# First stage of an attention and MLP kernel: V and two query groups projected in small tiles on both halves of the rows, scores among them; clears behind the first inverse root

## The chip, the cores and the metric

The kernel runs on one core of a Trainium2 chip. The metric is the device time of one execution in microseconds (us). TensorE (PE) does the matrix products, ScalarE (ACT) activations and copies, VectorE (DVE) reductions and elementwise work, GpSimd (POOL) elementwise work, and SyncE (SP) issues the transfers. Each engine works through its own queue in order.

## The reference

```python
# S = 2048 rows, D = 512, 32 heads of 16, F = 1792
xn = layernorm(A_x)                        # (x - mean) / sqrt(var + 1e-5)
q, k, v = split_heads(xn @ A_wqkv)
p = softmax(q @ k.T * 16 ** -0.5)
attn = merge_heads(p @ v) @ A_wo
mlp = gelu(xn @ B_w1 + B_b1) @ B_w2 + B_b2
out = A_x + attn + mlp
```

## The kernel before

A product that must be exact to about float32 is made of three products of float16 pairs (high and low part of each factor), so a tile of 128 x 512 with D = 512 takes 4 x 3 = 12 matmuls. The work falls into a first stage, a loop of units, and an end.

**The unit loop.** One unit belongs to a group of four heads and 512 queries (16 units each) and covers 128 keys; there are 512 units. PE makes the scores of the four heads first with queries as the weights (S, 128 x 512 each), of which DVE takes the maximum over the keys (L392, four to a unit); 16 units give the row maxima m of the 512 queries. Later PE makes the scores again with keys as the weights and with the row maxima in added rows of the stacks (E), ACT takes the exponential of E (L433, four instructions of 128 x 512 to a unit), and PE multiplies by V. The S part runs 19 units (`LEAD`) ahead of E. All these matmuls are small tiles of 62 or 64 rows by 32 columns (helper at L171), several of which run side by side in the array, on two halves of its rows. On the half of the rows that P·V leaves free runs "dense" work: the projections of the later head groups, the remaining V tiles, then the MLP, then the output projection. The last V tiles (11 to 15) are the first of that dense work.

**The first stage**, which the change rewrites, prepares this. A class `Plan` is a list scheduler: `add` puts down a task with its engine, a guessed duration in ns, what it comes after, the buffers that it takes and frees, and a `tail` (how much work hangs behind it); `run` takes at each step, for the engine that can start first, the startable task with the longest tail, and so fixes the order of every engine's queue. Its guesses are used for nothing else. The tasks, with the lines of before:

- `tile_in` (L900): the 16 tiles of x, 128 x 512 each, into 8 buffers; tiles 8 to 15 wait until earlier ones have been transposed. `wq_in` (L909): the first weights of Q and K. `piece_in` (L915): weight pieces of 512 KB (`wch`, three buffers): two of V, then 18 pieces m0 to m17 of the MLP and output weights.
- `total` (L923): ACT sums a piece's absolute values, from which scale factors are worked out; it frees the piece's buffer. The totals of the 18 pieces have the lowest tail of all.
- `normal`: mean and variance (L972, L973), `sd` = var + eps (L974), a Sqrt on ACT (L976), a Newton step on DVE (L978 to L982), then x is normalised, two tiles of the first four on DVE (L990) and two on ACT (L987).
- `turned`: PE transposes (L1004), copies to float16 high parts on ACT (L1008), low parts on DVE or POOL (L1017, L1023).
- `twelve` (L1034): the 12 full 128 x 128 x 512 matmuls of one tile, in four chunks of three. `project0` does so for a K or Q group of 512 rows, copies the result (`stg`), stores it (`qk_d`) and loads it back in stacked form (`kst`, `qst`, L538).
- `score`: two tasks to a unit, each eight small matmuls into two banks, then two maxima of 128 x 512 on DVE (L392).
- `v_tile`: `twelve` for one of the first 11 (`NV`) V tiles, copied by ACT to `vv` (L1131).
- the row maxima of the first 16 units: a reduction on DVE (L358), three small steps on POOL (L360 to L362), a PE transpose (L366), a copy on ACT (L371), a store by SP (`m_d`, L347) and two loads into the rows of `qst` (`m_rows`, L352).
- POOL clears `kst`, `qst` of both sets and parts of `vv` at the very start (L90, L93, L94).

While PE has nothing to do, `fill` gives it matmuls whose results are not used (L1192).

Of the kernel before, what the change touches and what calls it, by code (L numbers as in the profile page):

```python
# [9 lines left out]
F32 = mybir.dt.float32  # L10
# [26 lines left out]
TAIL = 5  # L37
WARM = 430
NV = 11
LAG, E_TAIL = 3000, 9500  # L40
LANE = 225
WFROM, WSTEP, XN = 10, 4.5, 4.5
VT = 2600, -2000
WV_TAIL, WV_DVE = 50000, 2
# [11 lines left out]
def layer_kernel(ctx: ExitStack, tc: tile.TileContext, x, wqkv, wo, w1, b1, w2, b2, out):  # L56
# [30 lines left out]
    def clear(i, blocks=range(NQB)):  # L87
        for b in blocks:
            for st, v in ((kst, MROWS), (qst, 0.0)):
                nc.gpsimd.memset(st[i][b].rearrange("p h n -> p (h n)").bitcast(F32), v)  # L90

    vv = const.tile([P, NT, H * VW + 15], F32, name="vv")
    nc.gpsimd.memset(vv[:, :, 0:H * VW].rearrange("p t (h e) -> p t h e", e=VW)[:, :, :, DH], 1.0)  # L93
    nc.gpsimd.memset(vv[:, :, H * VW:], 0.0)  # L94
# [122 lines left out]
    class Plan:  # L217
# [3 lines left out]
        def __init__(self, **pools):  # L221
            self.todo, self.pools = [], {k: (n, []) for k, n in pools.items()}
            self.freed, self.slot, self.users = {}, {}, {}

        def add(self, engine, ns, fn, after=(), take=(), free=(), size=0, tail=0, gap=0):
            t = dict(gap=gap, e=engine, ns=ns, fn=fn, after=[a for a in after if a], take=take, free=free, size=size, tail=tail,
                     end=None, n=len(self.todo))
            for key in free:
                self.users.setdefault(key, []).append(t)
            self.todo.append(t)  # L230
            return t

        def late(self, a, t):
            return 60 if a["e"] == t["e"] else self.LATE[a["e"]]
# [16 lines left out]
        def run(self, fill):  # L251
            for t in reversed(self.todo):
                for a in t["after"]:
                    assert a["n"] < t["n"]
                    wire = LAG + a["size"] * 3 if a["size"] else 0
                    a["tail"] = max(a["tail"], t["tail"] + max(t["ns"] + self.late(a, t) + wire, t["gap"] if a["gap"] else 0))
            at = {"PE": 1200.0, "ACT": 2020.0, "DVE": 1200.0, "POOL": 4000.0, "SP": 740.0}
            wire, left = 0.0, list(self.todo)
            while left:
# [7 lines left out]
                s, t = max((c for c in can[e] if c[0] <= first[e] + 120), key=lambda c: (c[1]["tail"], -c[1]["n"]))  # L267
                if e == "PE":
                    fill(at[e], s)
                for key in t["take"]:  # L270
# [5 lines left out]
                if t["size"]:  # L276
                    wire = max(wire, at[e] + 1300) + t["size"] * 3
                    t["end"] = wire + 500
# [75 lines left out]
    def m_parts(t):  # L354

        mx = work.tile([P, 2, 8], F32, name="mx", bufs=1)
        parts = work.tile([P, 2, 2, 8], F16, name="mparts", bufs=2)
        return (lambda: nc.vector.tensor_reduce(mx.rearrange("p a r -> p (a r)"), mt_of[t].rearrange("p h t k -> p (h t) k"),  # L358
                                                axis=AX.X, op=ALU.max),
                lambda: nc.gpsimd.tensor_scalar(mx, mx, 1.0 / MROW, 0.0, op0=ALU.mult, op1=ALU.add),  # L360
                lambda: nc.gpsimd.tensor_scalar(parts[:, :, 0], mx, 1.0, 0.0, op0=ALU.mult, op1=ALU.add),
                lambda: nc.gpsimd.tensor_tensor(parts[:, :, 1], mx, parts[:, :, 0], op=ALU.subtract)), parts  # L362
# [238 lines left out]
    def split_qk(m, wf, inv, ready_w):  # L601
        wh = ph.tile([P, 2, 2, NC, P], F16, name="wqk_h", bufs=2)
        for w in (1, 0):
            assert (m, w) in here
# [234 lines left out]
    with ExitStack() as st1:  # L839
# [53 lines left out]
        def raw(key, tag, shape, bufs):  # L893
            tl[key] = (px if tag == "xs" else ph).tile(shape, F32, name=tag, bufs=bufs)
            return tl[key]

        def tile_in(t):
            def fn():
                xs[t] = raw(("xs", t), "xs", [P, D], 8)
                nc.sync.dma_start(xs[t], x[t * P:(t + 1) * P, :])  # L900
            return add("SP", 450, fn, take=[("xs", t)], size=256, tail=(300000 if t < 4 else 270000 if t < 8 else 0))
# [10 lines left out]
        def piece_in(key, src, after=(), tail=0):  # L912
# [3 lines left out]
            return add("SP", 420, fn, after, take=[key], size=700, tail=tail)  # L916

        def total(ns, key, dst, after, done=()):
# [5 lines left out]
            return add("ACT", ns, fn, [after], free=done)  # L924
# [25 lines left out]

        amq = work.tile([P, 2], F32, name="amq")
# [10 lines left out]
        n_last = []  # L962
        DVE_X, DVE_LO = (2, 2, 0, 0), (4, 4, 0, 0)

        def normal(sb):
# [10 lines left out]
            a = add("ACT", 200, lambda: nc.scalar.activation(sd[:, 1], sd[:, 0], AF.Sqrt), [a] + n_last)  # L976
            n_last[:] = [a]
            a = add("DVE", 90, lambda: nc.vector.tensor_tensor(sd[:, 2], sd[:, 1], sd[:, 1], op=ALU.mult), [a])  # L978
            a = add("DVE", 90, lambda: nc.vector.tensor_tensor(sd[:, 2], sd[:, 2], sd[:, 0], op=ALU.add), [a])
            a = add("DVE", 90, lambda: nc.vector.reciprocal(sd[:, 3], sd[:, 2]), [a])  # L980
            a = add("DVE", 90, lambda: nc.vector.scalar_tensor_tensor(sd[:, 2], sd[:, 1], 2.0, sd[:, 3], op0=ALU.mult, op1=ALU.mult), [a])
# [12 lines left out]
        def turned(sb, done):  # L994

            his, los = [], []
            for c in range(NC):
# [8 lines left out]
                t = add("PE", 440, turn, done, take=[key], free=[("xs", 4 * sb + i) for i in range(4)])  # L1006
# [31 lines left out]
        def project0(w, sb):  # L1038

            key, st = ("X", "p", w, sb), ("stg", w, sb)  # L1040
            p = twelve(key, [lambda c=c, i=i, j=j: (wqh[:, w, i, c, :], xt[:, j, c, sb * QB:(sb + 1) * QB])
                             for c in range(NC) for i, j in PAIRS], lambda c: [his[sb][c], los[sb][c], w_ready[w], t_last[sb]])
# [5 lines left out]
            h = add("ACT", 480, hi, [p], take=[st], free=[key])  # L1048
# [14 lines left out]
            for a_ in range(2):  # L1063
                got.append(add("SP", 420, lambda a_=a_: stack(0, w, sb, a_), [a, b], size=96))
# [464 lines left out]
```

## Time and profile before

| | |
|---|---|
| median of 3 runs | 1450.94 us (1450.76 to 1452.97) |
| profiled execution | 1450.07 us, its span 1448.3 us |
| PE, DVE, ACT, POOL busy | 99%, 93%, 87%, 47% of the span |
| first score matmul | 33.53 us |
| last score matmul of the first stage | 94.80 us |
| first exponential of the unit loop | 95.48 us |
| last exponential | 1431.5 us |

Rows of the timeline give start, duration, engine, line, operation, output<-input and count; in brackets stands the idle time of the engine before it and what ended it. "SPq" is the issue of a transfer, "PEld" a weight load. A table of stretches has the stretch, its length, busy time and count of each engine (PE, PEld, DVE, ACT, POOL, or only the one asked for), the granted PE clock, the share of the DMA engines and GB/s. A row of waits has the waiting engine and line, what it waited for, the us in total, the times, and the longest.

### The profile page before, as it was taken

What the parts mean: (1) busy time and instruction counts of PE and PEld (TensorE: products, weight loads), DVE (VectorE), ACT (ScalarE), POOL (GpSimd) and SP (SyncE); (2) the same over time, 40 slices, a digit from 0 to 9 for tenths busy, and PEclk for the clock granted to TensorE, in tenths of its full rate; (3) what the DMA queues carried; (4) which work ended last, traced back from release to release, by engine and by line L of the source; (5) the groups of instructions that cost most, each with busy time, mean ns of one, the idle gap of its engine ahead of it and who ended that gap; (6) DMA issues with size and microseconds to landing.
All of it is one profiled execution on the core that took longest, in us unless ns stands there. A gap on an engine that the chain in (4) does not pass through costs nothing.

```text
span 1448.3 us, 88564 instructions
## 1 busy us (share of the span) xinstructions
PE 1430.8 (99%) x40120; PEld 960.0 (66%) x40120; DVE 1350.1 (93%) x2240; ACT 1259.7 (87%) x2399; POOL 684.6 (47%) x769
## 2 busy tenths in 40 slices
PE   7999999999999999999999999999999999999998
PEld 3347676766666667666677766666766667666664
DVE  7979999999999999999999999999999999999933
ACT  5868888888999888999998889998889999888885
POOL 3301857663688511278742137884015778212110
PEclk9999999999999999999999999999999999999999
DMA  6741564555224111121113011121112210211423
GB/s 210 216 139 33 171 205 159 160 177 158 73 87 120 55 47 38 46 84 45 45 45 89 24 45 45 53 77 46 44 36 73 62 37 21 59 56 47 137 70 115
DMA packets 111474, 124.84 MB, mean 86 GB/s; under 512 B 21244, under 2 KB 83068, under 8 KB 111096
## 3 DMA queue, kind: packets, MB, share of 16 engines
q1 hardware_dynamic: 111096, 119.18, 27.2%
q8 instruction: 313, 5.13, 1.5%
q14 instruction: 65, 0.53, 0.1%
HBM read 81.66 MB, written 37.34 MB: 82 GB/s over the span
## 4 chain that ended last, share of the span: by engine, by line
PE 93%; DVE 4%; ACT 1%; DMA 1%; issue 0%; POOL 0%; DVEq 0%; SPq 0%; ACTq 0%
PE pD L171 27%; PE pV L171 26%; PE pT L171 19%; PE pS L171 17%; DVE mt L392 3%; PE pT L1034 2%; PE pD L1034 1%; DMA wq<-in_A_wqkv_dram 0%; DMA xs<-in_A_x_dram 0%; ACT xs L987 0%; DVE xt L1017 0%; ACT pe L433 0%; DVE sd L974 0%; POOL xt L1023 0%; DVE ac L1404 0%
## 5 line engine op out<-in xcount | busy, mean ns | idle before, releaser
L392 DVE TENSOR_REDUCE mt<-pS 128x1 f32<-128x512 f32 x2029 | 1279.2, 683 | 36.5 <-PE pT L171 8.7
L433 ACT ACTIVATE pe<-pT 128x512 f32<-128x512 f32 x2048 | 1109.8, 599 | 143.6 <-PE pT L171 62.1
L171 PE MATMUL pV<-pe,vv 64*32 64x512 f32 x8192 | 1087.1, 591 | 0.1
L171 PE MATMUL pT<-qst,kst 64*32 64x512 f16 x8192 | 705.0, 378 | 0.9 <-ACT pf L644 0.4
L171 PE MATMUL pS<-kst,qst 62*32 62x512 f16 x8116 | 624.0, 378 | 1.3 <-DVE mt L392 1.2
L171 PEld LDWEIGHTS <-qst 62*32 62x32 f16 x8192 | 307.8, 91 | 194.1 <-issue 45.4
L171 PE MATMUL pD<-xb,wc 64*32 64x512 f16 x5376 | 363.1, 375 | 0.0
L171 PE MATMUL pD<-w_s,g 64*32 64x512 f16 x5376 | 360.8, 375 | 0.0
L171 PEld LDWEIGHTS <-kst 64*32 64x32 f16 x8192 | 279.5, 91 | 97.7 <-issue 23.6
L171 PEld LDWEIGHTS pV<-pe,vv 64*32 64x32 f32 x8192 | 240.2, 105 | 12.6 <-PE pV L171 4.4
L171 PEld LDWEIGHTS <-wc 64*32 64x32 f16 x5376 | 160.3, 91 | 44.7
L171 PEld LDWEIGHTS <-g 64*32 64x32 f16 x5376 | 162.3, 91 | 39.0
L171 PE MATMUL pD<-xt,wqk_h 64*32 64x512 f16 x2400 | 159.1, 376 | 0.0
L360 POOL TENSOR_SCALAR mx<-mx 128x16 f32<-128x16 f32 x32 | 6.5, 204 | 300.0 <-DVE mx L358 296.0
L1371 POOL TENSOR_TENSOR xa<-xa,yt 128x512 f32<-128x512 f32 x16 | 20.5, 1280 | 153.5 <-ACT yt L1369 153.5
L171 PEld LDWEIGHTS <-wqk_h 64*32 64x32 f16 x2400 | 73.3, 92 | 19.4 <-issue 0.2
L1323 POOL TENSOR_TENSOR t<-hh 128x512 f32<-128x512 f32 x56 | 58.2, 1040 | 41.3 <-ACT hh L1346 39.1
L1325 POOL TENSOR_TENSOR t<-t,hh 128x512 f32<-128x512 f32 x56 | 71.7, 1281 | 4.7
L1318 POOL TENSOR_TENSOR t<-t,hh 128x512 f32<-128x512 f32 x56 | 71.8, 1282 | 4.6
L1320 POOL TENSOR_TENSOR g<-t,g 128x512 f16<-128x512 f32 x56 | 65.2, 1164 | 4.7
L490 POOL TENSOR_TENSOR osb<-osb,rb 128x512 f32<-128x512 f32 x31 | 39.8, 1284 | 40.4 <-DMA rb<-den_d 34.2
L171 PE MATMUL pD<-wo_s,oc 64*32 64x512 f16 x816 | 54.6, 376 | 0.0
(160 smaller groups left out, 933.5 us busy)
## 6 DMA issues: line engine op xcount, KB each, us to landing
wc<-w_d SPq DMA_DIRECT2D x56, 256.0 KB
qk_d<-stg SPq DMA_DIRECT2D x32, 256.0 KB
rb<-den_d SPq DMA_DIRECT2D x124, 64.0 KB
wch<-in_B_w_dram SPq DMA_DIRECT2D x14, 512.0 KB
wch<-in_B_w_dram SPq DMA_DIRECT2D x28, 256.0 KB
w_d<-wsp SPq DMA_DIRECT2D x28, 256.0 KB
kst<-qk_d SPq DMA_DIRECT2D x64, 96.0 KB
qst<-qk_d SPq DMA_DIRECT2D x64, 96.0 KB
```

The lines of the kernel that those rows point to most:

```text
L171: p = nc.tensor.matmul(*args, **kw)
L360: lambda: nc.gpsimd.tensor_scalar(mx, mx, 1.0 / MROW, 0.0, op0=ALU.mult, op1=ALU.add),
L392: nc.vector.reduce_max(mt_of[t][:, n // 2 + n % 2 * 2, qt, kb:kb + 1], s, axis=AX.X)
L433: nc.scalar.activation(pe, st, AF.Exp, scale=scale_of[g // 2])
L490: pooled((1280, lambda: nc.gpsimd.tensor_tensor(osb, osb, rb, op=ALU.mult)), (620, lambda: nc.gpsimd.tensor_scalar(ot[:, 0], osb, 1.0, 0.0 ...
L1034: nc.tensor.matmul(tl[key], lhs, rhs, start=c + n == 0, stop=(c, n) == (NC - 1, 2))
L1318: (1280, lambda: nc.gpsimd.tensor_tensor(t1, t1, hh, op=ALU.mult)),
L1320: (1160, lambda: nc.gpsimd.tensor_tensor(g[:, 1, f, :], t1, g[:, 0, f, :], op=ALU.subtract)),
L1323: pooled((1040, lambda: nc.gpsimd.tensor_tensor(t1, hh, hh, op=ALU.mult)), (620, lambda: nc.gpsimd.tensor_scalar(t1, t1, 1.0, 1.0 / GELU_A ...
L1325: (1280, lambda: nc.gpsimd.tensor_tensor(t1, t1, hh, op=ALU.mult)),
L1371: add = lambda: nc.gpsimd.tensor_tensor(xa, xa, yt, op=ALU.add)
```

## The change

- x tiles 8 to 15 get eight buffers of their own (a tag of the exponentials' pool), so all 16 loads are issued at the start.
- The Sqrt on ACT becomes a power of -1/2 on POOL (L993 of after) with a Newton step on DVE. The Exp table is loaded once, at the start.
- The clears become tasks: those of set 0 and `vv` (ten) stand before the first power on POOL, those of set 1 (eight) right behind it.
- The K groups are projected by full-array matmuls in the order 0, 2, 1, 3. Then come seven pairs (`PAIRED`), each of two groups in 64 x 32 tiles: V tiles 0 to 11 and the Q groups 1 and 2. `side_by_side` runs one group on the upper and one on the lower half of the rows; at the middle they change halves, with a wait (`enter`, `leave`) between.
- The scores stand among these small tiles. One V tile more (12) is done in the first stage.
- The planner's costs are changed: a penalty for a change between full array and small tiles, a bonus for staying, and a hold on weight pieces (`BULK`, `HOLD`) while the wire is busy.

What that does at three places of the order. First SP, the end of the first stage; `wch` are the weight pieces (the last two are of wo), `m_d` is the store of the row maxima and `qst_0<-m_d` their loads. Before:

```order
L538 DMA kst_3_82<-qk_d 48x2x512 x2
L915 DMA wch<-in_B_w_dram 128x2x512 x4
L915 DMA wch<-in_A_wo_dram 128x2x512 x2
L1061 DMA qk_d<-stg 128x512
L347 DMA m_d<-mturned 64x64
L1060 DMA qk_d<-stg 128x2x512
L352 DMA qst_0_87<-m_d 2x4x256 x2
```

After:

```order
L549 DMA qst_2_89<-qk_d 48x2x512 x2
L929 DMA wch<-in_B_w_dram 128x2x512 x4
L358 DMA m_d<-mturned 64x64
L929 DMA wch<-in_B_w_dram 128x2x512
L363 DMA qst_0_87<-m_d 2x4x256 x2
L929 DMA wch<-in_B_w_dram 128x2x512 x2
L929 DMA wch<-in_A_wo_dram 128x2x512 x2
```

The last four pieces have moved from ahead of the row maxima to behind them.

On ACT, the same place; `vv` are the copies of V tiles, `wch,amx<-wch` the totals, `pe` the exponentials. Before:

```order
L1131 ACTIVATE vv<-pD 128x32x16
L371 ACTIVATE mturned<-pS 64x64
L923 ACTIVATE wch,amx<-wch 128x1024
L1131 ACTIVATE vv<-pT 128x32x16 x2
L433 ACTIVATE pe<-pT 128x512 x14
```

After:

```order
L382 ACTIVATE mturned<-pS 64x64
L937 ACTIVATE wch,amx<-wch 128x1024 x2
L1187 ACTIVATE vv<-pD 128x32x16
L1187 ACTIVATE vv<-pT 128x32x16
L937 ACTIVATE wch,amx<-wch 128x1024
L1187 ACTIVATE vv<-pT 128x32x16 x2
L937 ACTIVATE wch,amx<-wch 128x1024 x4
L444 ACTIVATE pe<-pT 128x512 x14
```

Where one total stood between the row maxima and the first exponential, seven stand now, four of them behind the last V copies.

On POOL, at the start; `kst` and `qst` with the ends 83 to 86 and 91 to 94 are set 1. Before:

```order
L90 MEMSET qst_2_93 128x512
L90 MEMSET kst_3_86 128x512
L90 MEMSET qst_3_94 128x512
L1099 TENSOR_SCALAR wq<-wq,invq_139 128x512
L1100 TENSOR_TENSOR wqk_h<-wq,wqk_h 128x512
```

After:

```order
L95 MEMSET qst_3_90 128x512
L993 TENSOR_TENSOR sd<-sd,power 128x4
L95 MEMSET qst_0_91 128x512
L95 MEMSET kst_0_83 128x512
L95 MEMSET qst_1_92 128x512
L95 MEMSET kst_1_84 128x512
L95 MEMSET qst_2_93 128x512
L95 MEMSET kst_2_85 128x512
L95 MEMSET qst_3_94 128x512
L95 MEMSET kst_3_86 128x512
L1153 TENSOR_SCALAR wq<-wq,invq_132 128x512
```

The power has come in, and eight of the clears now run behind it.

The diff, cut to its core:

```diff
+BULK, HOLD = 600, 1500
-NV = 11
+NV = 12
+PAIRED = (0, 1), (2, 3), (4, 5), ((0, 1), (0, 2)), (6, 7), (8, 9), (10, 11)
+SPLIT, SWITCH, SAME, KLAG = 4, 160, 1500, (0, 0, 12000, 12000)
...
@@ Plan.start
+            if t["size"] >= BULK:
+                s = max(s, self.wire - HOLD)
...
@@ Plan.run
-                s, t = max((c for c in can[e] if c[0] <= first[e] + 120), key=lambda c: (c[1]["tail"], -c[1]["n"]))
+                s, t = max((c for c in can[e] if c[0] <= first[e] + 120),
+                           key=lambda c: (c[1]["tail"] + (SAME if e == "PE" and c[1]["small"] == self.small else 0), -c[1]["n"]))
...
@@ first stage
-        clear(0)
-        plan = Plan(xs=8, stg=3, pf=2, wch=3, wq=2, S=4, X=4)
+        plan = Plan(xs=8, xp=8, stg=3, pf=2, wch=3, wq=2, S=4, X=4)
...
+        hot = work.tile([P, 1], F32, name="hot")
+        add("ACT", 300, lambda: nc.scalar.activation(hot, ident[:, 0:1], AF.Exp), tail=400000)
...
-            a = add("ACT", 200, lambda: nc.scalar.activation(sd[:, 1], sd[:, 0], AF.Sqrt), [a] + n_last)
...
+            r = add("POOL", 1030, lambda: nc.gpsimd.tensor_tensor(sd[:, 1], sd[:, 0], power, op=ALU.pow), [a])
...
+        def side_by_side(*groups):
+            last = None
+            for k in range(2):
+                for c in range(NC):
+                    def fn(k=k, c=c):
+                        if c == 0:
+                            if k:
+                                enter()
+                            else:
+                                for key, _, _ in groups:
+                                    xbank(key)
+                        for n in range(3):
+                            for user, side, (key, prods, _) in zip("VD", (k, 1 - k), groups):
+                                lhs, rhs = prods[3 * c + n]()
+                                r = slice(64 * side, 64 * side + 64)
+                                tiled(user, tl[key], lhs[r], rhs[r], k + c + n == 0, (k, c, n) == (1, NC - 1, 2))
+                        if c == NC - 1:
+                            for user in "VD":
+                                leave(user, not k)
...
+        for sb in range(1, NQB):
+            k_ready[sb] = project0(1, sb)
+        for pair in PAIRED[:SPLIT]:
+            two(*pair)
+        for u in range(16):
+            score(u)
...
-            add("SP", 270, lambda k=k: m_rows(0, k), [put], size=4, tail=E_TAIL)
-        for t in range(NV):
-            v_tile(t)
-        q_ready[2] = project0(0, 2)
+            add("SP", 660, lambda k=k: m_rows(0, k), [put], size=4, tail=E_TAIL)
+        for pair in PAIRED[SPLIT:]:
+            two(*pair)
```

More of the change, by code (lines that the diff above doesn't have):

```diff
@@ L923, in fn @@
                 nc.scalar.activation(o, v, AF.Abs, scale=1.0 / SPREAD, accum_out=dst)
-            return add("ACT", ns, fn, [after], free=done)
+            return add("ACT", ns, fn, after if isinstance(after, list) else [after], free=done)
         def scale_chain(am, n, after, name):
@@ L1004, in turn @@
                         nc.tensor.transpose(tl[key][:, i * P:(i + 1) * P], xs[4 * sb + i][:, c * P:(c + 1) * P], ident)
-                t = add("PE", 440, turn, done, take=[key], free=[("xs", 4 * sb + i) for i in range(4)])
+                t = add("PE", 440, turn, done, take=[key], free=[x_key(4 * sb + i) for i in range(4)])
                 hi, lo = xt[:, 0, c, cs], xt[:, 1, c, cs]
@@ L1152, in layer_kernel @@
         for step in m_steps[1:]:
-            a = add("POOL", 220, step, [a])
+            a = add("POOL", 230, step, [a])
         def turn_m():
```

140 lines of the change are left out of this document (82 added, 58 removed).

## The prediction, on record before the changed kernel was timed

> **What bounds the kernel now.** I read the page first: busy times, then the chain, then the costliest groups.
>
> ```profile
> span 1448.3 us, 88564 instructions
> PE 1430.8 (99%) x40120; PEld 960.0 (66%) x40120; DVE 1350.1 (93%) x2240; ACT 1259.7 (87%) x2399; POOL 684.6 (47%) x769
> ...
> PE 93%; DVE 4%; ACT 1%; DMA 1%; issue 0%; POOL 0%; DVEq 0%; SPq 0%; ACTq 0%
> ...
> L392 DVE TENSOR_REDUCE mt<-pS 128x1 f32<-128x512 f32 x2029 | 1279.2, 683 | 36.5 <-PE pT L171 8.7
> L433 ACT ACTIVATE pe<-pT 128x512 f32<-128x512 f32 x2048 | 1109.8, 599 | 143.6 <-PE pT L171 62.1
> ```
>
> The program is one long PE chain: PE stands in 93% of the chain that ended last, and DVE's maxima of the scores (2029 reductions, 1279 us) run just below it. So a gain in the first stage counts only by how much earlier the unit loop starts, which I read as the first exponential (L433 on ACT). A table of stretches, and one restricted to L433, give the loop's own pace:
>
> ```profile
> 106.00:380.00 274.00, 222.03 (x408) 1.00 0.48 147
> 400.00:1370.00 970.00, 811.86 (x1502) 1.00 0.20 57
> 1390.00:1430.00 40.00, 32.83 (x61) 1.00 0.24 77
> ```
>
> There are four exponentials to a unit, so 274.0/(408/4) = 2.69 us per unit in the first phase, 970/(1502/4) = 2.58 in the middle and 40/(61/4) = 2.62 at the end. The change moves one V tile ahead of the loop, and in the order every later phase begins three units sooner; the number of units is the same. What is left of that is three units at 2.62 for three at 2.69: -0.2 us. The V tile's own products ran in the loop beside the P·V matmuls on the other row half, so taking them out frees no other PE time.
>
> The timeline around the loop's start tells what the first exponential waited for:
>
> ```profile
> 79.09 0.37 SPq L915 DMA_DIRECT2D wch<-in_B_w_dram  x1
> 80.87 2.85 SPq L915 DMA_DIRECT2D wch<-in_A_wo_dram  x2
> 83.49 1.06 ACT L923 ACTIVATE wch<-wch 128x1024 f32<-128x1024 f32 x1 [0.16 <-DMA wch<-in_B_w_dram]
> 87.28 0.22 DVE L358 TENSOR_REDUCE mx<-mt 128x16 f32<-128x64 f32 x1
> 87.59 0.20 POOL L360 TENSOR_SCALAR mx<-mx 128x16 f32<-128x16 f32 x1 [23.00 <-DVE mx L358]
> 88.84 1.05 ACT L923 ACTIVATE wch<-wch 128x1024 f32<-128x1024 f32 x1
> 88.98 0.53 SPq L347 DMA_DIRECT2D m_d<-mturned  x1
> 89.79 0.20 ACT L923 ACTIVATION_READ_ACCUMULATOR wch<-wch 128x1 f32 x1
> 92.59 1.46 SPq L352 DMA_DIRECT2D qst<-m_d  x2
> 94.80 0.40 PE L171 MATMUL pV<-kst,qst 62*32 62x512 f16 x4
> 94.91 0.60 ACT L1131 ACTIVATE vv<-pT 128x512 f32<-128x512 f32 x1 [2.88 <-PE pT L1034]
> 95.04 0.39 PE L171 MATMUL pT<-qst,kst 64*32 64x512 f16 x4
> 95.48 0.60 ACT L433 ACTIVATE pe<-pT 128x512 f32<-128x512 f32 x1
> 96.59 0.41 PE L171 MATMUL pS<-kst,qst 62*32 62x512 f16 x8 [1.16 <-DVE mt L392]
> SPq L915 <- ACT wch L923: 8.1, 5, 2.2
> SPq L352 <- DMA m_d<-mturned: 2.4, 1, 2.4
> ```
>
> The last 512 KB weight pieces are issued by SP at 80.87 and 83.36 (two in the row of 2.85 us, the second ending with it). ACT sums the last one at 88.84, long before it is wanted. Then the row maxima go out (m_d at 88.98) and come back (issued 92.59). The last scores at 94.80, the last V copy at 94.91, the first E matmul at 95.04 and the first exponential at 95.48 stand close together: PE, m rows and ACT all end near 95. Behind them PE waits for DVE, which is still reducing (96.59, 1.16 us idle). SP's issues of the pieces already wait for ACT's sums (five times, 8.1 us): a piece may only be fetched when the sum three pieces earlier has freed its buffer.
>
> **The change, part by part.**
>
> *All x loads at the start.* At present x tiles 8 to 15 wait for buffers, and the fourth K group comes so late that DVE stands still:
>
> ```profile
> 30.78 1.84 SPq L900 DMA_DIRECT2D xs<-in_A_x_dram  x4
> 33.53 0.61 PE L171 MATMUL pS<-kst,qst 62*32 62x512 f16 x12
> 77.59 1.89 DVE L392 TENSOR_REDUCE mt<-pS 128x1 f32<-128x512 f32 x3 [5.07 <-PE pS L171]
> ```
>
> With buffers of their own (those that later hold the exponentials, first written at 95.48) the late tiles load with the early ones, and the 5.07 us of DVE idle time ahead of 77.59 can go. I add no more than that. Eight loads more, 256 KB each, now stand on SP ahead of the second Q/K weights and the first stacks: at 1.84/4 = 0.46 us of issue each that is 3.7 us of the queue, which is through long before the first stack is asked for; hidden, and if the wire is not done by then, at most those 3.7 us on the first score.
>
> *Square root on POOL, one Exp table load, clears behind it.* These rows of the first 16 us bear on it:
>
> ```profile
> 2.93 0.52 POOL L90 MEMSET kst<- 128x512 f32 x1
> 8.07 2.40 DVE L974 TENSOR_SCALAR sd<-mv 128x4 f32<-128x4 f32 x1
> 8.77 1.28 ACT L976 ACT_TABLE_LOAD   x1
> 9.92 0.52 POOL L90 MEMSET qst<- 128x512 f32 x1
> 10.50 0.20 ACT L976 ACTIVATE sd<-sd 128x4 f32<-128x4 f32 x1 [0.45 <-DVE sd L975]
> 11.62 0.54 DVE L990 TENSOR_SCALAR xs<-xs,mv,sd 128x512 f32<-128x512 f32 x1
> 6.30:11.40 5.10, 0.00 (x0) 0.00 (x0) 4.59 (x11) 2.82 (x6) 4.14 (x9) 0.75 1.06 349
> 11.40:15.00 3.60, 3.54 (x11) 1.90 (x12) 2.07 (x10) 3.26 (x6) 0.00 (x0) 0.50 0.52 192
> 77.00:95.50 18.50, 18.43 (x173) 6.17 (x173) 16.38 (x28) 10.71 (x22) 1.79 (x4) 1.00 0.54 171
> ```
>
> The step sd of L974 was held from 8.07 to 10.47, until the run of POOL clears ended at 10.44 (9.92 + 0.52), and the Sqrt then waited for a table load too. After the change eight clears and two of vv stand before the power; ten instead of eighteen, so POOL is free at about 10.44 - 8 x 0.465 = 6.7 (their distance below), before sd is asked for at 8.07: -2.4. The power on POOL has no row; the nearest one, a small POOL op at L360, takes 0.20, and the plan's own table puts 1.03 for it, against 0.20 for the Sqrt; I take 1.0, since a power is more than a multiply, so +0.8. The Newton step is two DVE ops shorter (-0.4). Eight further clears follow the power, at (9.92 - 2.93)/15 = 0.465 apart 3.7 us in all, just when DVE does the two TENSOR_SCALARs that normalise (L990, 0.54 each now): if they are held as L974 was, +1.5 to +3.7 comes back; half the tiles are normalised on ACT, and the weight scale runs beside. I take the first score 2.5 us earlier (the range is 0 to 3.6).
> The Trainium skill, "SBUF — State Buffer", section "Who interferes with whom", says that DVE and GpSimd share one port pair under an exclusive lock, that a tensor_scalar can enter the mode that takes it, and that a reduction never does; the 2.40 us at L974 beside the clears agrees. By that rule the normalising steps would be held for the whole run of clears, and the 2.5 would become about 0.
>
> *Small tiles in place of full-array products.* Between a full-array chunk and the scores PE now loses time at each turn:
>
> ```profile
> 44.67 0.11 PEld L171 LDWEIGHTS <-qst 62*32 62x32 f16 x8 [0.42 <-issue]
> 44.67 0.41 PE L171 MATMUL pS<-kst,qst 62*32 62x512 f16 x8
> 45.78 0.11 PEld L171 LDWEIGHTS <-qst 62*32 62x32 f16 x8 [0.42 <-issue]
> ```
>
> One chunk of three and one pair of score tiles take 45.78 - 44.67 = 1.11 us. Three matmuls at about 0.215 are 0.645 and eight small ones on the array side by side about 0.215, so 0.25 is lost per cycle. The 19 units of scores are 38 pairs of tiles, and all but the first few stand between chunks; with 30 cycles it is 7.5 us of PE time. Against it the extra V tile costs 12 x 0.215 = 2.6, and each of seven pairs changes row halves behind a wait at its middle (up to 0.25 each, 1.8). PE gains 3 to 5 us.
> DVE's maxima set a second limit: 76 tiles at 0.605 are 46 us, while the scores now take from 33.53 to 95.2. So both limits leave room. For the last score I sum: -2.5 (start) - 5.1 (K3 idle) + 2.6 (V tile) = -5.0: at 89.8, and PE is through with the last V pair, which stands behind the last scores, at about 91.5.
>
> *The queue at the end.* The rewritten order does something else, and this decides my forecast. On SP the m rows (L352, now L363) come before the last four weight pieces, not behind them. On ACT the last four sums stand between the last V copies and the first exponential. Take the max of m 5.0 earlier: 82.3. From there to the issue of the m rows took 92.59 - 87.28 = 5.3: 87.6. Two rows take 1.46: 89.0. Then pieces 14 to 16 are issued. From issue to the sum that waited for it the piece of 79.09 took until 83.49, 4.4 us: 93.4. Its sum and read take 1.05 + 0.20, which frees the buffer: 94.7. Only then can the last piece, 17, be issued; alone on the wire I let it take 3.5 to 4.4, an estimate from the 4.4 with others in flight: 98.2 to 99.1. Its sum ends at 99.4 to 100.3. The same by ACT: V copies at 91.5 + 2 x 0.6 = 92.7, then sum 14, then a load: 92.7 + 1.25 + 3.5 + 1.25 = 98.7. Lower end 98.7, upper 100.3; I take 99.2, since pieces lie apart there as they did at 80.87 and 83.36. So the first exponential moves from 95.48 to 99.2: +3.7, though the scores end 5 us sooner.
>
> *What comes back.* In units 0 to 2 DVE is behind now, and the first three units take longer than the pace, as the fourth unit's first exponential shows:
>
> ```profile
> 105.68 1.09 ACT L433 ACTIVATE pe<-pT 128x512 f32<-128x512 f32 x2 [0.71 <-PE pS L171]
> ```
>
> From 95.48 to 105.68 is 10.2 us where 3 x 2.62 = 7.9 would do. After the change DVE has finished by 91.5 and the scores of the lead lie ready, so up to 2.3 comes back; I take 2.0.
>
> Sum against the profiled execution (1448.3 span, 1450.07 in all, so 1.8 around it): +3.7 - 2.0 - 0.2 = +1.5, or 1451.6. The median of the runs, 1450.94, stands 0.87 above the profiled one: 1452.4. From this kernel's runs (1450.76 to 1452.97) 0.2%, 2.9 us, is about what a measurement can tell from no change, so this is "the same": 1449 to 1454 as the own range of this case.
>
> **The rivals.**
>
> *The pieces don't hold the exponential (faster).* If SP gets pieces 14 to 17 out about 6 us sooner than I work out (the first 16 units' maxima done by 77, or the pieces landing in far less than 4.4 us), ACT is free when the scores end. The first exponential then follows them as now: 95.48 - 5.0 = 90.5, and with -0.2 the time is 1450.94 - 5.2 = 1445.7. The point that decides it is the issue of piece 17 before about 87. For it speaks that ACT has spare time (10.71 busy of 18.5 us in the row 77.00:95.50); against it that SP takes its queue in order, with the m rows ahead.
>
> *PE goes cold in the gap, and the clears hold DVE (slower).* PE would have nothing but one unit's E between 93 and 99. In the rows above PE stood still from 6.3 to 11.4 and then ran at a granted clock of 0.50 from 11.4 to 15.0. The same at 99, with PE the bound, costs half of some 3.6 to 7 us of work: +1.8 to +3.5. With the start not gained (+2.5 on all that follows) the time is 1452.4 + 2.5 + 1 = 1456; with the clock alone 1454.9. It decides if the gap is longer than about 4 us.
> The Trainium skill, "TensorE: Matmul & The Clock Gate", section "What's actually happening", puts the drop to half after an idle window of about 3.4 us; the trace agrees (5.1 us idle, then 0.50). By that rule the gap of some 5 us would bring it.
>
> *Small tiles are no faster than the full array (the change does not do what it says).* If the two row halves don't overlap, a pair of groups takes twice its 5.2 us; seven pairs would add 36 us, and the time would be 1480. The main loop's P·V and dense matmuls run on two halves today at the pace shown, so I give this 0.02.
>
> **How the numbers follow.** The own case (first exponential near 99, most of it won back) 0.42; no hold by the pieces 0.25, and all of that counts as faster, with 0.02 from the better part of the own case; the cold PE or the held start 0.29 and no overlap 0.02, both slower. A time 0.2% faster needs the first exponential below about 95. Faster 0.27, same 0.42, slower 0.31. The range leaves out one in ten at either side: below 1445.5 a gain beyond that of the scores, above 1456 the sum of both slow rivals.
>
> **What would show it.** In the profile after: first score near 31 and last near 90; DVE's idle time before the fourth K block's scores gone; POOL's power about 1 us long, DVE's normalising steps 0.54 if not held; the scores and V tiles without the 0.42 issue gaps; SP's last weight piece issued near 94 and ACT's last sum ending near 99; the first exponential right behind that sum, PE idle for 4 to 6 us ahead of it, and the next three units about 2.7 us apart; granted clock below 1 behind the gap if the slow rival holds. I am wrong if the last sum ends before the last score, or if the loop's start is not where the time goes.

## The result: 1.1% slower, and the profile after

The changed kernel takes 1468.11 us in the median (1463.71 to 1471.15, four runs) against 1451.72 us (1450.76 to 1452.97): ratio 1.011, 95% interval 1.0082 to 1.0138. The forecast was 1452.4 with a range up to 1456; the measured time, 16.4 us above that of the kernel before, lies outside it. Three executions, one of the kernel before (8375.27 us), one of e1 (5231.41) and one of e12 (2974.01), lie far outside the others and count in no median or ratio here.

The profiled execution of the changed kernel is its slowest, 1471.15 us. Its page:

```profile
span 1469.4 us, 90770 instructions
PE 1440.3 (98%) x41229; PEld 974.2 (66%) x41229; DVE 1348.5 (92%) x2236; ACT 1257.0 (86%) x2394; POOL 689.4 (47%) x774
...
PE 90%; DVE 4%; DMA 2%; ACT 1%; issue 1%; SPq 1%; POOL 0%; POOLq 0%; DVEq 0%; ACTq 0%
```

PE was 93% of the chain that ended last and is 90%; DMA has grown to 2%, and "issue" and SPq have 1% each. The span has grown by 21.1 us, more than the 16.4 between the medians. The first exponential comes 11.6 us later than before (107.06 against 95.48), and the loop from there to the last unit's first exponential takes 1346.0 instead of 1336.0 us, 10.0 more; what comes after it is 0.4 shorter. (The 1431.5 in the table ahead is the last unit's first exponential.) So there are two places to look at.

**The start of the loop.** Timeline of the changed kernel around it:

```profile
97.20 5.12 SPq L929 DMA_DIRECT2D wch<-in_A_wo_dram  x2
99.81 1.08 ACT L1187 ACTIVATE vv<-pT 128x512 f32<-128x512 f32 x2 [2.63 <-PE pT L174]
100.78 1.06 ACT L937 ACTIVATE wch<-wch 128x1024 f32<-128x1024 f32 x1
106.00 1.06 ACT L937 ACTIVATE wch<-wch 128x1024 f32<-128x1024 f32 x1 [1.73 <-DMA wch<-in_A_wo_dram]
107.06 1.06 ACT L444 ACTIVATE pe<-pT 128x512 f32<-128x512 f32 x2
107.69 0.61 PE L174 MATMUL pT<-qst,kst 64*32 64x512 f16 x4 [5.54 <-ACT pe L444]
```

The last two pieces are issued in the row of 97.20; the second of them starts at 101.95 and ends that row, since it needs the buffer that the sum of 100.78 frees, and that sum stands behind the V copies of 99.81. ACT then waits 1.73 us for the piece, sums it at 106.00, and only then takes the exponential, for which PE waits 5.54 us. This is the hold that the prediction described. But the V copies themselves, which need PE's last products, end at 100.9, where the prediction had 92.7. Before, they ended at 95.5; so of the 11.6 us at the start 5.4 are PE's lateness and 6.2 the hold.

What made PE late stands in its waits ahead of the first exponential, and in two rows of its timeline:

```profile
PE pT L174 <- issue: 4.0, 3, 2.0
PE pS L174 <- issue: 1.8, 1, 1.8
66.08 0.39 PE L174 MATMUL pT<-wvh,xt 64*32 64x512 f16 x2 [2.00 <-issue]
85.65 0.39 PE L174 MATMUL pS<-kst,qst 62*32 62x512 f16 x2 [1.78 <-issue]
```

Four times PE stood for 0.67 to 2.0 us with nothing to wait for that the profile shows, 5.8 us in all. The granted clock fell behind the first of them, as a row of the table of stretches shows (length, PE, PEld, DVE, ACT and POOL busy, granted clock, DMA share, GB/s):

```profile
66.60:70.00 3.40, 3.40 (x80) 1.78 (x71) 1.29 (x2) 1.76 (x4) 0.00 (x0) 0.50 0.41 136
```

Before, no such wait of PE stands in the first stage. The transfers of the queue that loads instructions, between 30 us and the first exponential, of the changed kernel and then of the kernel before (count, MB, share):

```profile
q8 instruction: 14, 0.23, 1.2%
```
```profile
q8 instruction: 4, 0.07, 0.4%
```

Fourteen loads of instructions instead of four: a full-array matmul has become eight small ones, on a wire that the weight pieces keep busy (a DMA share of 0.65 from 60 to 90 us). The trace ties the waits to these loads: the four ended at 66.08, 80.00, 85.65 and 97.38, each 1.3 to 1.5 us after a load had ended (64.81, 78.61, 84.38, 95.85). The table of stretches of the changed kernel shows what the gap ahead of the first exponential left behind:

```profile
104.00:106.00 2.00, 0.00 (x0) 0.00 (x0) 0.00 (x0) 0.27 (x2) 0.00 (x0) 0.54 1.05 351
108.00:110.00 2.00, 2.00 (x32) 0.88 (x29) 0.00 (x0) 1.09 (x3) 0.00 (x0) 0.50 0.00 0
112.00:114.00 2.00, 2.00 (x32) 0.85 (x23) 1.29 (x2) 1.08 (x2) 0.00 (x0) 0.50 0.00 0
116.00:118.00 2.00, 2.00 (x66) 1.28 (x58) 1.92 (x4) 1.28 (x3) 0.00 (x0) 1.00 0.00 0
```

The granted clock was 0.50 from 106 to 114, while PE had work from 107.69 on.

**The loop.** The first stretch of 16 units lasts 46.1 us (45.1 before), the second 49.4 (43.7 before). In it stands a wait that was not there:

```profile
161.74 0.72 ACT L154 ACTIVATE wqk_h<-wq,inv 128x512 f16<-128x512 f32 x1 [3.38 <-DMA wq<-in_A_wqkv_dram]
162.99 0.61 PE L174 MATMUL pT<-qst,kst 64*32 64x512 f16 x4 [2.24 <-ACT pe L444]
```

ACT waits 3.38 us for the Q/K weights of the next group, with the exponentials queued behind that instruction, so PE waits for ACT, and a row of four matmuls takes 0.61 again, where 0.39 is usual. Before, the same step (L151) had no wait:

```profile
151.02 0.72 ACT L151 ACTIVATE wqk_h<-wq,inv 128x512 f16<-128x512 f32 x1
```

Besides, the last units hold one interval of 4.50 us, in which PE waits 1.21 us for a load of the last outputs; no other kernel here shows that interval.

### The profile page after: what moved, and what is told of

It reads as the page before. It is cut to its first block, busy times and chain, and to the rows that moved or that the text cites. A ratio compares the mean times of both kernels' runs of the same rounds, so it can differ in the third digit from the quotient of the medians.

```text
span 1469.4 us, 90770 instructions
## 1 busy us (share of the span) xinstructions
PE 1440.3 (98%) x41229; PEld 974.2 (66%) x41229; DVE 1348.5 (92%) x2236; ACT 1257.0 (86%) x2394; POOL 689.4 (47%) x774
## 4 chain that ended last, share of the span: by engine, by line
PE 90%; DVE 4%; DMA 2%; ACT 1%; issue 1%; SPq 1%; POOL 0%; POOLq 0%; DVEq 0%; ACTq 0%
PE pD L174 27%; PE pV L174 26%; PE pT L174 21%; PE pS L174 16%; DVE mt L403 3%; DMA wq<-in_A_wqkv_dram 1%; PE pT L1049 0%; PE pD L1049 0%; DMA wch<-in_A_wo_dram 0%; ACT pe L444 0%; DMA rb<-den_d 0%; DMA den_d<-dn 0%; DVE wvh L1171 0%; DMA ot_d<-ot 0%; ACT pe L1002 0%
## 5 line engine op out<-in xcount | busy, mean ns | idle before, releaser
L444 ACT ACTIVATE pe<-pT 128x512 f32<-128x512 f32 x2048 | 1109.1, 599 | 150.2 <-PE pT L174 66.6
L174 PE MATMUL pS<-kst,qst 62*32 62x512 f16 x8116 | 630.8, 379 | 1.9 <-issue 1.8
L174 PEld LDWEIGHTS <-qst 62*32 62x32 f16 x8192 | 312.0, 91 | 184.9 <-issue 36.2
L371 POOL TENSOR_SCALAR mparts<-mx 128x16 f16<-128x16 f32 x32 | 6.6, 206 | 303.0 <-DVE mx L369 303.0
L174 PEld LDWEIGHTS <-wqk_h 64*32 64x32 f16 x2592 | 78.6, 93 | 25.0 <-issue 6.2
```

The costliest lines, as they stand in the source:

```text
L174: p = nc.tensor.matmul(*args, **kw)
L371: lambda: nc.gpsimd.tensor_scalar(parts[:, :, 0], mx[:, 0], 1.0 / MROW, 0.0, op0=ALU.mult, op1=ALU.add),
L444: nc.scalar.activation(pe, st, AF.Exp, scale=scale_of[g // 2])
```

## The experiments

All times in one table. "First exp." is the start of the first exponential, "loop" the time from it to the first exponential of the last unit, both in the profiled execution, which is one alone: e4, e6, e7 and e9 have the same order on ACT, DVE, POOL and SP throughout the loop, and their loops differ by up to 7.8 us.

| kernel | median us | ratio to before (95%) | first exp. | loop |
|---|---|---|---|---|
| before | 1451.72 | | 95.5 | 1336.0 |
| changed | 1468.11 | 1.0110 (1.0082 to 1.0138) | 107.1 | 1346.0 |
| e1 11 V tiles | 1465.53 | 1.0093 (1.0078 to 1.0107) | 109.0 | 1339.9 |
| e2 no hold on pieces | 1466.94 | 1.0090 (1.0072 to 1.0107) | 105.3 | 1348.8 |
| e3 full array | 1457.88 | 1.0045 (1.0031 to 1.0059) | 100.4 | 1340.1 |
| e4 all three | 1451.17 | 0.9997 (0.9986 to 1.0007) | 94.2 | 1339.6 |
| e5 narrow pieces | 1457.12 | 1.0036 (1.0024 to 1.0048) | 97.7 | 1343.2 |
| e6 two small pairs | 1449.11 | 0.9984 (0.9975 to 0.9993) | 94.6 | 1335.5 |
| e7 late clears | 1448.63 | 0.9985 (0.9976 to 0.9995) | 93.5 | 1334.3 |
| e8 before, 12 V tiles | 1461.15 | 1.0066 (1.0050 to 1.0081) | 98.1 | 1343.8 |
| e9 e6 and e7 | 1445.40 | 0.9953 (0.9938 to 0.9967) | 92.9 | 1331.8 |
| e10 last four narrow | 1465.88 | 1.0087 (1.0065 to 1.0110) | 105.8 | 1342.1 |
| e11 without the last four | 1462.18 | 1.0067 (1.0050 to 1.0083) | 100.4 | 1344.7 |
| e12 three small pairs | 1448.54 | 0.9976 (0.9968 to 0.9985) | 96.7 | 1336.3 |

**e1, 11 V tiles in the first stage.**

```diff
-NV = 12
+NV = 11
-..., (8, 9), (10, 11)
+..., (8, 9), (10,)
```

> The changed kernel with 11 V tiles in the first stage instead of 12, so that every phase of the loop begins at the unit where it began in the kernel before; the last V tile of the first stage is alone on its row halves, so PE has about the same time to spend there. Theory (the loop's two late stalls come from phases that begin three units sooner, while the transfers that they need are issued at the same unit as before): the 6.63 us unit at the second group of 16 and the 4.50 us unit at the end go, the loop gets 6 to 8 us shorter, the first exponential stays at 104 to 108; time 1459 to 1463 against 1468. Rival (the stalls come from the late start, which pushes SP's queue against the units): the intervals stay above 4 us, and the time is within 2 us of the changed kernel's.

The units 17 to 19 went from 6.63, 3.97 and 4.04 us to at most 2.8, and ACT's wait for the weights is gone, though the loop began 2 us later than in the changed kernel. The loop is 6.0 us shorter, as the theory said: the second stretch of 16 units takes 43.2 instead of 49.4. The 4.50 us interval of the last units is gone too, but another of 4.71 us has come 24 units earlier, with an unnamed wait of PE of 1.09 us. The time missed the forecast, in part because the first exponential came at 109.0. Why is open: PE's unnamed waits were 6.0 us, hardly more than the 5.8 of the changed kernel. The intervals of the two times overlap; what shows the twelfth tile's price is the wait itself, and e8.

**e2, no hold on the pieces.**

```diff
-BULK, HOLD = 600, 1500
+BULK, HOLD = 10 ** 9, 1500
```

> The changed kernel without the planner's hold on weight pieces: in the new order two pieces fewer stand behind the loads of the row maxima, only the last one. Theory (the first exponential waits for the last weight sum): it comes as much sooner as that sum does, 4 to 6 us, and with it the whole run: first exponential 101 to 103, time 1462 to 1464. Rival (PE's own stalls for instructions set the start, because the scores end at 100 either way): first exponential not before 105 and the time within 2 us.

A miss, with the rival borne out: the first exponential came 1.7 us sooner, not 4 to 6, and the time moved by 1.2 us, well within the spread. PE's unnamed waits were 8.0 us, the last scores ended at 104.6, and the last sum at 105.4. The longest of the waits:

```profile
81.38 0.39 PE L174 MATMUL pT<-wvh,xt 64*32 64x512 f16 x2 [3.16 <-issue]
```

With the pieces earlier the wire is fuller while PE needs its instructions (a DMA share of 1.03 from 70 to 80 us, against 0.70 in the changed kernel): taking away one delay fed the other.

**e3, full-array products for the pairs.**

```diff
-            p = side_by_side(*(v_group0(k) if isinstance(k, int) else qk_group(*k) for k in which))
             for k in which:
+                p = twelve(*(v_group0(k) if isinstance(k, int) else qk_group(*k)))
```

> The changed kernel with each of the seven pairs projected by full-array matmuls one after the other, as before, all else as changed (12 V tiles, hold, power on POOL, x buffers). PE has about 1200 rows ahead of the first E instead of 3560. Theory (the small tiles need three times the instructions, and PE stands waiting for them, 5.8 us in four stalls of 0.7 to 2.0): the stalls marked issue of PE above 0.6 us go, the last scores end 3 to 6 us sooner than 100.4, or the mode switches take that back; the first exponential follows the last weight sum, 101 to 105; time 1461 to 1467. Rival (the stalls are of the wire and come with any order): PE still stands for 4 us or more in stretches marked issue ahead of the first E.

No wait of PE marked issue of 0.6 us or more is left ahead of the first exponential, which comes 6.7 us sooner, behind the last sum; PE does not go cold (granted clock 1.00 in the 12 us after it). Instruction loads in that stretch:

```profile
q8 instruction: 4, 0.07, 0.5%
```

Four, as before. The long units 17 and 18 stay (6.60 and 3.88 us): they have nothing to do with the small tiles. The 10 us that this wins are most of the loss. But they are not PE's alone: the last V copy ends at 99.47, only 1.4 us sooner than in the changed kernel. With other tasks the planner also puts the last two pieces out at 93, and the last sum runs beside the V copies instead of 5 us behind them:

```profile
93.04 0.90 SPq L929 DMA_DIRECT2D wch<-in_A_wo_dram  x2
97.92 1.55 ACT L1187 ACTIVATE vv<-pT 128x512 f32<-128x512 f32 x3
99.35 1.06 ACT L937 ACTIVATE wch<-wch 128x1024 f32<-128x1024 f32 x1
```

So e3 took away both delays at once. It does not show that the mode switches are cheaper than the small tiles: from the first score to the last V copy it takes 69.1 us, the changed kernel with its waits 70.3, and e5 below, small tiles without the waits, 62.7.

**e4, the three together.** The edits of e1, e2 and e3.

> All three at once: 11 V tiles, full-array products, no hold; what remains of the change is the x buffers, the power on POOL with the clears behind it, the early Exp table and the order of the K groups. Theory: the weight sums no longer stand behind the last V copies, the loop's stalls are gone; first exponential at 92 to 95 and time 1446 to 1451. Rival (the start itself, with its clears and x loads, costs as much as it gains): first exponential at 95.5 or later and 1451 or more.

First exponential 94.2, as the theory said; the time, 1451.17, is just above the theory's 1446 to 1451 and is that of the kernel before. The last piece is out at 84.1 here, and the first exponential directly follows the V copies. All of the loss lay in these three parts together; the x buffers, the power, the table load and the K order are left, and bring 1.3 us at the start. The loop is 3.6 longer in this execution; one unit of 4.70 us holds a wait of PE marked issue of 1.14 us.

**e5, the changed kernel with pieces of an eighth.**

```diff
-                nc.sync.dma_start(tl[key], src)
+                nc.sync.dma_start(*((tl[key], src) if tail else (tl[key][:, :1, :P], src[:, :1, :P])))
```

and the sums take the same part.

> The changed kernel with every one of the 18 weight pieces of the MLP and output weights cut to 64 KB (an eighth), loads and sums alike, in the same order; the scale factors then come from a part of the weights only. PE's program is the same. Theory (PE stands because its instructions, fetched over the same wire as the weights, come late while the wire is full): with the wire free the stretches of PE marked issue above 0.6 us go (5.8 us before), the last scores end at 94 to 96 instead of 101, the sums hold nothing, PE does not go to half clock; first exponential at 95 to 97, loop still with the stall near unit 17 unless the wire was its cause. Time 1452 to 1458. Rival (small tiles need instructions faster than they can be fetched at all): the stalls stay at 4 us or more, and the scores end after 99.

PE's program is the same, and the instruction loads are as many; but the waits marked issue are gone. The first two rows are PE's longest waits ahead of the first exponential, the third the instruction loads:

```profile
PE pT L1021 <- DVE xt L1034: 1.1, 1, 1.1
PE pT L1051 <- POOL xt L1040: 0.8, 1, 0.8
q8 instruction: 14, 0.23, 1.4%
```

So it takes both, many instructions and a busy wire (a DMA share of 0.25 from 60 to 90 us here, 0.65 in the changed kernel). The last scores start at 94.28 instead of 101.75: 7.5 us, which is the 5.8 of the waits and, by estimate, the 1.7 that 3.4 us at half clock cost. Still, against the forecast, the last sum holds the first exponential to 97.7, and the granted clock falls to 0.50 behind it:

```profile
97.39 0.31 ACT L939 ACTIVATE wch<-wch 128x128 f32<-128x128 f32 x1 [3.10 <-DMA wch<-in_A_wo_dram]
97.70 1.55 ACT L444 ACTIVATE pe<-pT 128x512 f32<-128x512 f32 x3
```

**e10 and e11, the hold by itself.** e10 cuts only the last four pieces to an eighth; e11 leaves them out, loads and sums, and sets their maxima to a constant:

```diff
+        nc.vector.memset(amx[:, 12:16], 1.0)
-        for n, src in enumerate(every[:NM]):
+        for n, src in enumerate(every[:NM - 4]):
```

> The changed kernel with only the last four weight pieces cut to 64 KB (an eighth), which are those that the new order puts behind the row maxima; their scale factors come from a part of the weights. The first 14 pieces and PE's program are as changed, so PE's waits for instructions stay. Theory (two delays add in the changed kernel: the scores end some 5 us later than before because PE waits for instructions, and the last sums add another 4 to 6): first exponential 100 to 102 instead of 107, no 5 us gap of PE ahead of it; time 1461 to 1464. Rival (the sums only fill time in which PE is late anyway): first exponential not before 105.

> The changed kernel without the last four weight pieces: neither loaded nor summed in the first stage, their maxima set to a constant. Everything ahead of the row maxima is as changed, and PE's program too. Cutting the pieces to an eighth left the last one 3.5 us from its issue to its sum, so that did not take the hold away; this does. Theory (the sums behind the last V copies hold the first exponential by themselves): it follows the V copies directly, at 100 to 102, without the 5 us gap, and PE stays at full clock; first exponential 5 us and time 5 to 8 us below the changed kernel: 1459 to 1463. Rival (something else, the row maxima or the scores, holds the exponential just as long): not before 105, time within 2 us of 1468.

e10 missed, and its first exponential, 105.8, is where the rival put it: the last piece, cut to 64 KB, was still issued only when a sum behind the V copies had freed its buffer, and ACT waited for it as before:

```profile
101.91 0.33 SPq L929 DMA_DIRECT2D wch<-in_A_wo_dram  x1
105.48 0.31 ACT L939 ACTIVATE wch<-wch 128x128 f32<-128x128 f32 x1 [3.02 <-DMA wch<-in_A_wo_dram]
```

The hold is of order and latency, not of bytes. e11 took it away, and the exponential follows the V copies directly:

```profile
99.44 1.08 ACT L1187 ACTIVATE vv<-pT 128x512 f32<-128x512 f32 x2 [2.65 <-PE pT L174]
100.41 1.80 ACT L444 ACTIVATE pe<-pT 128x512 f32<-128x512 f32 x3
```

107.06 - 100.41 = 6.65 us at the start, of which 0.4 is that the V copies end sooner, and the clock stays at 1.00; the time is 5.9 us below that of the changed kernel, as forecast. So e10's rival does not hold.

**e8, the kernel before with 12 V tiles.**

```diff
-NV = 11
+NV = 12
...
-            assert (m, w) in here
+            while (m, w) not in here:
+                yield
```

The second part, which the changed kernel has too, lets the split of the next group's weights wait until their load has been issued.

> The kernel before with 12 V tiles in the first stage instead of 11, nothing else changed (the split of the next weights waits for their load to be issued, as in the changed kernel). Theory (the phases that begin three units sooner meet weights of the next group not yet landed): first exponential 2.6 us later, at about 98, and a stall at units 17 to 19 of 3 to 5 us with half clock behind it; time 1456 to 1460. Rival (that stall needs the late or crowded start of the changed kernel): only the 2.6 us, 1453 to 1455.

The first exponential comes 2.6 us later, as counted, and the time is 0.66% longer: the stall comes with the twelfth tile, without anything else of the change's first stage.

```profile
152.65 0.72 ACT L151 ACTIVATE wqk_h<-wq,inv 128x512 f16<-128x512 f32 x1 [4.21 <-DMA wq<-in_A_wqkv_dram]
153.90 0.62 PE L171 MATMUL pT<-qst,kst 64*32 64x512 f16 x4 [4.37 <-ACT pe L433]
```

ACT waits 4.21 us for the weights of the next group, PE then 4.37 for ACT, and matmuls take 0.62 behind it. The loads of these weights are issued in unit 16, as before (145.3 here, 143.2 before), but the step that needs them comes in unit 17 instead of 19. The loop is 7.9 us longer, and the time is above the forecast: 5.1 us lie in the second stretch of 16 units, with the stall, and 2.6 between units 64 and 128, whose cause is open. Over all the runs unit 17 takes 5.9 to 7.5 us in each of the seven kernels with 12 V tiles and 2.6 to 2.8 in each of the seven with 11.

**e7, clears of set 1 later (on e4).**

```diff
-            add("POOL", 720, lambda k=k: clear(1, [k]), tail=-9000)
+            add("POOL", 720, lambda k=k: clear(1, [k]), [staged[1, 3]], tail=-9000)
```

> e4 with the eight clears of set 1 taken from behind the first power to behind the last low parts on POOL, some 30 us later. Theory (clears hold DVE's tensor_scalar steps only for the rest of one clear, not for the run of them): the two normalising steps on DVE take 1.07 instead of 1.37 together, the scale step 0.17 instead of 0.55, and the first score comes 0.5 to 1 us sooner than 29.8; the time does not change (within 1.5 us of e4). Rival (the clears cost the start several us): first score before 28, time 2 us or more below e4.

The scale step and the two normalising steps on DVE, first beside the clears (the changed kernel), then without (e7):

```profile
10.84 0.55 DVE L961 TENSOR_SCALAR facq<-sc_c 128x2 int32<-128x2 int32 x1
11.50 1.37 DVE L1005 TENSOR_SCALAR xs<-xs,mv,sd 128x512 f32<-128x512 f32 x2
```
```profile
10.79 0.17 DVE L961 TENSOR_SCALAR facq<-sc_c 128x2 int32<-128x2 int32 x1
11.07 0.99 DVE L1005 TENSOR_SCALAR xs<-xs,mv,sd 128x512 f32<-128x512 f32 x2
```

The scale step is 0.38 us shorter, the two normalising steps together 0.38, and the first score comes 0.7 sooner, as forecast. The Trainium skill, "SBUF — State Buffer", section "Who interferes with whom", has one instruction hold the port pair for its whole length: the run here agrees, 0.38 is less than one clear of 0.52, and not the run of eight. In the kernel before, the step of L974 was held for 2.40 us, longer than one clear; what decides between the two is not shown. The time, 1448.63, is 2.5 us below e4's, where at most 1.5 were forecast; the start explains 0.7 of it, and the intervals of the two overlap.

**e6, e12 and e9, a better kernel.** e6 is e4 with the first two pairs in small tiles, which run from 40 to 62 us, when the first eight of the 18 pieces are issued; e12 has three pairs and the late clears; e9 is e6 with the late clears.

```diff
+            both = which in PAIRED[:2] and side_by_side(*(v_group0(k) for k in which))
             for k in which:
-                p = twelve(...)
+                p = both or twelve(...)
```

> e4 with only the first two pairs, V tiles 0 to 3, in small tiles side by side, which run at 40 to 55 us, where the transfers are few; the rest in full-array products. Theory: two or three more fetches of instructions, at a time when the wire is half empty, cost little, and some mode switches go: first exponential 0.5 to 2 us before that of e4 (94.2), time 1449 to 1451. Rival (any small tiles cost fetches): a stall of 1 us or more marked issue among them, no gain or up to 2 us lost.

> e6 and e7 together: 11 V tiles, no hold, small tiles for the first two pairs only, the clears of set 1 some 30 us later. If the two gains add (hybrid pairs 1 to 2 us at the start, clears 0.7), the first exponential is at 92.5 to 94 and the time 1447 to 1449, under both kernels; if they are the same gain seen twice, or only the spread of PE's waits for instructions, it is within 0.1% of e6 and e7.

> e9 with three pairs of V tiles in small tiles instead of two; the third runs when the weight pieces load. Theory (mode switches saved against PE waiting for instructions while the wire is full): a stall of 0.7 us or more marked issue comes back and eats the gain: first exponential 92.5 to 94.5, time 1445 to 1448. Rival (small tiles pay as long as most of the stage is full-array): first exponential below 92, time below 1445.

e6 has no unnamed wait of PE in the first stage, with seven instruction loads, though its DMA share was 0.68 from 40 to 60 us: the mean share alone does not tell when PE has to wait, and how busy the wire must be stays open. Its first exponential is 0.4 us later than e4's, not sooner; the 2 us of its time lie in the loop, so what the two pairs bring at the start is not shown by it. In e12 the third pair brings the wait back, as the theory said:

```profile
PE pV L174 <- issue: 2.1, 1, 2.1
```

and the first exponential comes at 96.7, later than forecast. e9 is the fastest, 0.47% below the kernel before (0.33 to 0.62%) and below its own forecast of 1447 to 1449:

```profile
span 1441.1 us, 89257 instructions
92.90 0.60 ACT L444 ACTIVATE pe<-pT 128x512 f32<-128x512 f32 x1
```

In the profiled execution 2.6 us of the gain are at the start and 4.2 in the loop, which has no interval above 3.31 us here. The loop's order on ACT, DVE, POOL and SP is that of e4, whose loop took 1339.6; PE's unnamed waits in the loop are 0.2 us here and 1.8 in e4. What made it shorter was not tried apart.

## Why the prediction was wrong, by its steps

For the first step, a stretch of the kernel before that holds the 5.07 us in which DVE stood ahead of 77.59 (columns as above):

```profile
72.50:77.60 5.10, 5.10 (x38) 2.10 (x36) 0.03 (x2) 3.34 (x7) 0.00 (x0) 1.00 0.90 269
```

- *The last score at 89.8, PE through at 91.5.* This step failed. The start was right in size (first score at 30.63, 2.9 us sooner, forecast 2.5, though the terms listed for it, -2.4, +0.8 and -0.4, add up to -2.0), but the sum had no term for PE's own instructions. Eight times as many matmuls of the same work, on a busy wire, cost 5.8 us of waits in the profile and some 1.7 of half clock; in e5, without them, the last scores come 7.5 us sooner. And even in e5 they start at 94.3, not 89.8: the 5.07 us of DVE idle time were added as a gain though PE was the bound of that stretch, busy for all 5.10 us of the row above.
- *The last weight sums hold the first exponential.* Right in its mechanism, wrong in its place. The sum stands directly ahead of the exponential, and e11 prices it at some 6 us. From the V copies at 92.7 the prediction's chain gave 98.7; from the measured 100.9 the same 6.0 gives 106.9, and 107.06 was measured. Nearly the whole error at the start, 107.1 instead of 99.2, is that of the step before.
- *Three units' shift of the phases, -0.2 us.* This failed worst for its size: e8 gives +5.1 us for it in the second stretch of 16 units, and +7.9 in the loop. The prediction took the loop as three units of one pace for three of another, and did not ask what ACT's queue meets sooner: a step whose weights are issued in the same unit as before.
- *What comes back, -2.0.* In e11, where PE does not go cold, 10.2 - 8.6 = 1.6 us came back in the first three units. In the changed kernel they took 11.2, 1.0 more than before: the half clock that one rival named took it all, 11.2 against 8.6.
- *The rival of the cold PE and the held DVE* gave the right sign, and the clock fell as it said, to 0.50, but this is 2.6 us of the 16. DVE was held for 0.4 us at a time, not for the run of clears.
- *The power*: 1.03 us, as taken.
- *Small tiles no faster*: this did not come about. From the first score to the last V copy e5 takes 62.7 us, e8 with the same tiles in full-array products, in another order, 64.5. The 36 us of this rival would have made 1487, not 1480.

## What to carry over

When matmuls are cut into small tiles, count the instructions too: their loads share the wire with the data. With two pairs alone in small tiles (e6) seven loads gave no wait, but a gain from it is not shown. Moving work out of a loop also moves every later phase of that loop; for each step that comes sooner ask when its transfer is issued. A chain of buffer, load and sum that stands in a queue ahead of the critical instruction costs its latency; cutting the transfer to an eighth shortened it from 4.1 to 3.6 us.

## What the runs showed of the hardware

- PE can stand for up to 3.2 us (e2) with no semaphore to blame, when instructions and data share the wire: 14 loads of 16 KB with weight pieces beside them gave four waits, 14 beside pieces of an eighth none, four beside whole pieces none. In six kernels all 27 such waits of 0.3 us or more in the first stage ended 1.2 to 1.5 us after a load had ended.
- A load of 64 KB took 3.6 us from its issue to its sum (101.91 to 105.48 in e10), hardly less than the 4.1 us of the 512 KB in its place in the changed kernel (101.95 to 106.00).
- Gaps of PE of 4.37 us (e8) and 5.54 us (the changed kernel) were followed by a granted clock of 0.50 and rows of four matmuls of 0.61 and 0.62 us instead of 0.39. So was the 2.24 us gap at 162.99 (PE was busy for 2.13 of the 4 us from 158 to 162), and the 2.00 us wait at 66.08: 0.50 from 66.6 to 70.0.
